# An attention and two-MoE kernel: first layer over pairs of groups, early attention products in four banks, k maximum by a tree, and all steps in one fixed list

## The chip, the cores and the metric

One core of a Trainium2 chip. The metric is the device time of one execution in microseconds (us), and the time of a kernel is the median of its runs. Five engines work side by side and wait for one another by semaphores: PE (TensorE, matmuls), DVE (VectorE), ACT (ScalarE), POOL (GpSimd) and SP (SyncE, which here issues nearly all DMAs, one after the other).

## What is computed

```python
# attention: q, k, v are 4 x 8 heads x 576 x 64, softmax of q over d, of k over the sequence
q_s = softmax(q, over d);  k_s = softmax(k, over seq)
x   = q_s @ (k_s.T @ v)                  # -> 2304 tokens x 512
# first MoE layer
h   = x @ w_in                           # 512 x 2048
g   = s * relu(h)**2 + b
x2  = g @ w_out                          # 2048 x 512
# second MoE layer: 8 experts, at most 576 tokens each, in token order
e   = argmax(x2 @ w_gate);  p = softmax weight of e
out = p * (relu(x2 @ w1[e]) @ w2[e])     # 0 for tokens over the capacity
```

## The kernel before

The 2304 tokens go in 9 groups of 256 (`G`), d_ff in 16 slices of 128 (`NF`). For the accuracy of fp32, every large product is three matmuls on high and low parts: high weight by high x, high weight by low x, low weight by high x. So each of the 16 slices of `w_in` and of `w_out` is loaded by SP (`load_w`, L181 and L186) and *converted*, in place, by six steps: `cv_abs` on ACT (L210), `cv_low` on DVE (L192), `cv_sign` on ACT (L202) or, for the slices listed in `bv`, on DVE (L200), `cv_join` on DVE (L215), `cv_hi` on ACT (L222) and `cv_lo` on DVE (L226).

**Attention.** For each of 4 batches and 4 pairs of heads: `load_k`, `k_max` (DVE, L351), transpose and maximum over partitions (`k_T` PE L358, `k_cm` DVE L364, `k_bc` PE L369), `k_sub` (DVE, or POOL for the pairs in `kpool`, L381), `k_exp` (ACT), the product k_s^T v (`k_kv`, PE L400), and the block `kvb` (`k_rec`, `k_blk`). For each group of tokens: `q_max`, `q_sub` (POOL), `q_exp`, `q_sum`, `q_norm` (POOL), transposes by PE (`q_T` L492, `q_Te`), `x1_mm` (PE, L507) for each half of the 512 columns, and its high and low parts `x1h`, `x1l` (`x1_hi` ACT L515, `x1_lo` DVE L521). In PSUM there are four banks of tag "x2", two of "h" and two of "a"; `x1_mm` uses an "a" bank.

**First MoE.** A unit is two blocks of 256 columns in one bank: for groups 0 and 1 the slices 2j and 2j+1 of one group, the two groups by turns; then group 2 alone, group 3 alone, and so on. `h_unit` is the first layer of a unit, 24 matmuls of 256 columns (L543 to L545). Then `h_relu` (ACT), `h_sq` (DVE), `h_hi` (ACT), `h_lo` (DVE), and two units later `x2_unit`, 12 matmuls of 512 columns (L609 to L611). Groups 0 to 3 (`NS`) get both layers. Groups 4 to 8 keep g and get the gate from `w_out` times `w_gate`, made once by the steps `w_add`, `w_tr`, `w_mm`, `w_x`, `w_sum`, `w_asm`, `w_shift`; x2 is then computed for tokens that are kept only (`x2_kept`, a branch).

**Second MoE.** The router's steps `r_*` give each token its slot. The first expert's weights are fetched ahead, and its first 256 tokens (part A) go through `gemm1_ahead` (L860 to L862) while the last group is routed. After that: the transposes of part B (`xpose_B`, PE L825), `gemm1` of part B, beside it the list of the other experts (`make_list`, some 25 small DVE steps) and the conversion of w2 (`conv2`, L782, by DVE and POOL in turn), then `gemm2` of both parts and the next expert. Nine DMAs fill the output with zeros (`zero_out`, L126).

What sets the order: every step has a rank, from its slot in a plan and hundreds of offsets (`PAR['d']`, `PAR['t']`). `arrange` (L1501) picks, engine by engine, the ready step that its model of costs lets start first, and emits the steps in that order; each engine then runs its own in that order. Where PE would wait, `arrange` puts idle matmuls (`warm`, L1599). What comes after the last `x2_kept` is written out by hand (L1626 to L1661).

Of the kernel before, what the change touches and what calls it, by code (L numbers as in the profile page):

```python
# [26 lines left out]
def kernel(ctx, tc, q, k, v, w_in, w_out, s_in, b_in, w_gate, w1, w2, cap, out, dbg=None):  # L27
    nc = tc.nc
# [29 lines left out]
    const = ctx.enter_context(tc.tile_pool(name="const", bufs=1))  # L58
# [198 lines left out]
    def w_mm(g, x2):
        if "ps" not in wx:
            wx["ps"] = ps_x.tile([P, 4, P], F32, tag="x2", name="pswg")
        for x in (x2, x2 + 1):  # L260
# [86 lines left out]
    def k_max(b, j):  # L347
        t = kt[b, j]
        p = P if b else P0
        m = at.tile([P, 2, D], F32, tag="rt", name="m1", bufs=2)  # L350
        nc.vector.tensor_reduce(out=m[:p], in_=t[:p].rearrange("p h r d -> p h d r"), axis=AX.X, op=ALU.max)  # L351
        kx[b, j] = m[:p].rearrange("p h d -> p (h d)")
# [147 lines left out]
    def x1_mm(n, hf):  # L500
        tt = qT.pop((n, hf))
        ps = ps_a.tile([P, 2, G], F32, tag="a", name="psx1")
        for i in range(2):
            for off, ln, b, s in runs(n):
                for r in range(2):
                    z = slice(r * D, (r + 1) * D)
                    nc.tensor.matmul(  # L507
                        ps[z, i, off:off + ln], kvb[b % 3][2 * hf + i][z], tt[z, i, off:off + ln],
                        start=True, stop=True, tile_position=(r * D, r * D),
                    )  # L510
        x1[n, hf] = ps
# [12 lines left out]
    def plan_q(n, s):
# [1215 lines left out]
```

## Time and profile before

| | |
|---|---|
| median of 3 runs | 563.48 us (562.38 to 563.79) |
| the profiled execution | 564.76 us, its span 563.0 us |
| PE busy | 539.3 us, 96% of the span |
| DVE, ACT, POOL busy | 320.6, 238.4, 132.6 us |
| HBM traffic | 59.97 MB, 107 GB/s over the span |

The profiled execution is 1.28 us above the median. Busy PE is not PE at its peak: idle matmuls and matmuls at a lower clock count as busy. The shares are means over stages with different limits, so the stages are read one by one.

### The profile page before, as it was taken

The page shows a single profiled execution, that of the slowest core. Times are in us where ns is not written, and L with a number is a line of the kernel's source. Part 1 is how long each engine was busy: PE and PEld are TensorE (multiplying, and loading weights), DVE is VectorE, ACT ScalarE, POOL GpSimd, SP SyncE. Part 2 cuts the span into 40 slices and gives each one's busy share as a digit, 9 for nine tenths or more (in the row PEclk, how much of TensorE's full clock was granted, in tenths as well). Part 3 has the DMA queues.
Part 4 walks back from the last instruction along what each step waited for, and adds up shares of the span by engine and source line. Part 5 has one row for each costly group of instructions (what it writes and reads, how often), then busy time and mean ns, then how long its engine had stood idle before and what let it go on. Part 6 is the DMA issues. An engine that isn't in the chain of part 4 may idle for free. (4 is left out here: it accounts for less than half of the span.)

```text
span 563.0 us, 10853 instructions
## 1 busy us (share of the span) xinstructions
PE 539.3 (96%) x4165; PEld 474.9 (84%) x4165; DVE 320.6 (57%) x735; ACT 238.4 (42%) x417; POOL 132.6 (24%) x184
## 2 busy tenths in 40 slices
PE   8999999999999999999999999999999878999993
PEld 8879988988888898888987989998899866899762
DVE  4999999993665575367464353473364557073010
ACT  2699898873423253224323322222352344162120
POOL 3400013122655222141211121140040206210111
PEclk9999999999999999999999999999999898999997
DMA  9996911314100652510100010103031899423101
GB/s 266 357 323 204 390 38 31 77 48 137 44 21 1 169 146 52 119 23 30 33 17 2 20 41 13 27 2 114 2 99 43 250 327 358 155 76 113 40 19 33
DMA packets 83333, 59.97 MB, mean 107 GB/s; under 512 B 40191, under 2 KB 75647, under 8 KB 83264
## 3 DMA queue, kind: packets, MB, share of 16 engines
q1 hardware_dynamic: 81104, 54.08, 31.7%
q0 software_dynamic: 2160, 5.01, 2.7%
q8 instruction: 39, 0.64, 0.5%
q14 instruction: 30, 0.25, 0.2%
HBM read 46.64 MB, written 12.51 MB: 105 GB/s over the span
## 5 line engine op out<-in xcount | busy, mean ns | idle before, releaser
L543 PE MATMUL psh<-x1h,wi 128*128 128x256 f32 x576 | 169.4, 294 | 1.3 <-PEq L644 0.7
L544 PE MATMUL psh<-x1l,wi 128*128 128x256 f32 x576 | 163.2, 283 | 0.3 <-DVE x1l L521 0.3
L545 PE MATMUL psh<-x1h,wi 128*128 128x256 f32 x576 | 162.9, 283 | 0.0
L543 PEld LDWEIGHTS psh<-x1h,wi 128*128 128x128 f32 x576 | 110.2, 191 | 9.3 <-issue 7.2
L544 PEld LDWEIGHTS psh<-x1l,wi 128*128 128x128 f32 x576 | 110.5, 192 | 1.0 <-DVE x1l L521 0.5
L545 PEld LDWEIGHTS psh<-x1h,wi 128*128 128x128 f32 x576 | 110.3, 191 | 0.0
L609 PE MATMUL psx<-wo,gh 128*128 128x512 f32 x128 | 52.0, 406 | 0.0
L573 DVE SCALAR_TENSOR_TENSOR rt<-rt,sb_s 128x512 f32<-128x512 f32 x44 | 36.8, 836 | 26.5 <-ACT rt L565 26.5
L610 PE MATMUL psx<-wo,gh 128*128 128x512 f32 x128 | 50.3, 393 | 0.0
L611 PE MATMUL psx<-wo,gl 128*128 128x512 f32 x128 | 50.1, 391 | 0.0
L565 ACT ACTIVATE rt<-psh 128x512 f32<-128x512 f32 x44 | 26.3, 599 | 56.2 <-PE psh L545 53.1
L247 POOL TENSOR_TENSOR wS<-wo 128x128 f32<-128x128 f32 x64 | 31.7, 526 | 30.6 <-DVE wT L254 30.6
L565 ACT ACTIVATE rg<-psh 128x512 f32<-128x512 f32 x28 | 16.6, 598 | 45.7 <-PE psh L545 36.7
L762 POOL DMA_INDIRECT mapd<-rpay,rslot x18 | 18.9, 1052 | 49.5 <-DMA mapd<-rpay,rslot 19.4
L573 DVE SCALAR_TENSOR_TENSOR rg<-rg,sb_s 128x512 f32<-128x512 f32 x28 | 20.9, 752 | 16.5 <-ACT rg L565 16.5
L466 POOL TENSOR_TENSOR qt<-qt,qm 128x512 f32<-128x512 f32 x14 | 17.6, 1277 | 48.7 <-DVE qm L458 34.3
L782 DVE TENSOR_TENSOR W<-raw,W 128x512 fp32r<-128x512 f32 x28 | 22.6, 830 | 11.0 <-ACT W L781 10.3
L609 PEld LDWEIGHTS psx<-wo,gh 128*128 128x128 f32 x128 | 24.3, 190 | 5.3 <-issue 1.0
L611 PEld LDWEIGHTS psx<-wo,gl 128*128 128x128 f32 x128 | 24.1, 188 | 5.3
L351 DVE TENSOR_REDUCE m<-kt 128x128 f32<-128x640 f32 (+1 forms) x16 | 21.6, 1352 | 11.2 <-DMA kt<-in_k 8.3
L610 PEld LDWEIGHTS psx<-wo,gh 128*128 128x128 f32 x128 | 24.2, 189 | 4.3 <-DVE wo L226 0.3
L959 POOL DMA_INDIRECT out<-y,mp x11 | 10.6, 965 | 70.4 <-ACT y L958 56.8
(226 smaller groups left out, 1113.3 us busy)
## 6 DMA issues: line engine op xcount, KB each, us to landing
ri<-in_moe_w_in SPq DMA_DIRECT2D x16, 512.0 KB, 8.2
ro<-in_moe_w_out SPq DMA_DIRECT2D x16, 512.0 KB, 10.1
raw<-in_moe_w SPq DMA_DIRECT2D x12, 512.0 KB, 5.8
raw<-in_moe_w SPq DMA_DIRECT2D x24, 256.0 KB, 4.9
out<-zero SPq DMA_DIRECT2D x9, 512.0 KB, 6.4
kt<-in_k SPq DMA_DIRECT2D x12, 256.0 KB, 3.1
vt<-in_v SPq DMA_DIRECT2D x24, 128.0 KB, 2.8
x2d<-zero SPq DMA_DIRECT2D x5, 512.0 KB, 3.3
```

What stands on the lines that cost most here:

```text
L247: nc.gpsimd.tensor_tensor(t[:, c], hi, lo, ALU.add)
L351: nc.vector.tensor_reduce(out=m[:p], in_=t[:p].rearrange("p h r d -> p h d r"), axis=AX.X, op=ALU.max)
L543: nc.tensor.matmul(ps, wt[:, 0, o], xh[:, c % 2], start=(c == 0), stop=False)
L544: nc.tensor.matmul(ps, wt[:, 0, o], xl[:, c % 2], start=False, stop=False)
L545: nc.tensor.matmul(ps, wt[:, 1, o], xh[:, c % 2], start=False, stop=(c == NC - 1))
L565: nc.scalar.activation(t, ps, AF.Relu)
L573: nc.vector.scalar_tensor_tensor(t, t, sb_s, t, op0=ALU.mult, op1=ALU.mult)
L609: nc.tensor.matmul(ps, gh[:, i, o], wt[:, 0], start=(f == 0), stop=False)
L610: nc.tensor.matmul(ps, gh[:, i, o], wt[:, 1], start=False, stop=False)
L611: nc.tensor.matmul(ps, gl[:, i, o], wt[:, 0], start=False, stop=(f == NF - 1))
L762: nc.gpsimd.indirect_dma_start(out=mapd[:, :], out_offset=bass.IndirectOffsetOnAxis(ap=slot[:, t:t + 1], axis=0), in_=pay[:, t], in_offset ...
L782: eng.tensor_tensor(dst[:, 1], src, dst[:, 0].bitcast(F32), ALU.subtract)
```

## The change

- **Pairs of groups.** For groups 0 to 3 a unit is one slice of `w_in` by two groups: `h_unit` is 12 matmuls of 512 columns. `x1h` and `x1l` of two groups lie in one tile (three buffers each). The first unit needs the x1 of groups 0 and 1; `x2_unit` holds four banks at a time.
- **Start.** `x1_mm` of groups 0 and 1 takes "x2" banks. SP loads k before q, and two k tiles of the next batch early. `k_max` is three `tensor_tensor` steps (L356 to L358).
- **Conversions.** 13 signs by DVE instead of 9; 10 `k_sub` on POOL instead of 6. `w_mm` in four parts in "a" banks.
- **One fixed list.** `arrange` takes the steps in the order of `PAR['seq']`. The list now also has what was written by hand: the evictions of part A's `gemm1_ahead`, the transposes of part B, its `gemm1_B0`, the making of the list, `conv2_0`, and the next expert's fetch and gather. The `zero_out` DMAs stand early.
- **End.** The last `gemm2` of part A of the second expert is held in a bank, and its output is written in both branches that follow; the experts after the second ("rest") are one general path.

```diff
+    XB = 3
+    PAIRED = (0, 1, 2, 3)
+    half_of = {n: n % 2 if n in PAIRED else 0 for n in range(NG)}
...
-        m = at.tile([P, 2, D], F32, tag="rt", name="m1", bufs=2)
-        nc.vector.tensor_reduce(out=m[:p], in_=t[:p].rearrange("p h r d -> p h d r"), axis=AX.X, op=ALU.max)
+        m = at.tile([P, 3, 2, D], F32, tag="rt", name="m1", bufs=2)[:p]
+        t = t[:p].rearrange("p h r d -> p r h d")
+        x = 2 if b else 3
+        nc.vector.tensor_tensor(m[:, 0:x], t[:, 0:x], t[:, x:2 * x], ALU.max)
+        nc.vector.tensor_tensor(m[:, 0], m[:, 0], m[:, 1], ALU.max)
+        nc.vector.tensor_tensor(m[:, 0], m[:, 0], t[:, 4] if b else m[:, 2], ALU.max)
...
-        ps = ps_a.tile([P, 2, G], F32, tag="a", name="psx1")
+        ps = ps_x.tile([P, 2, G], F32, tag="x2", name="psx1") if n < 2 else ps_a.tile([P, 2, G], F32, tag="a", name="psx1")
...
     def x1_hi(n, hf):
-        xh = at.tile([P, 2, G], F32R, tag="x1h", name="x1h", bufs=4)
-        nc.scalar.activation(xh, x1[n, hf], AF.Copy)
+        z = half_of[n]
+        if z == 0:
+            shape = [P, 2, 2 if n in PAIRED else 1, G]
+            xs[n, hf] = [at.tile(shape, F32R, tag=f"x1{y}", name=f"x1{y}", bufs=XB) for y in "hl"]
+        xs[n, hf] = xs[n - z, hf]
+        nc.scalar.activation(xs[n, hf][0][:, :, z], x1[n, hf], AF.Copy)
...
     def h_unit(u, pair):
-        for i in range(2):
-            h_half(u, pair, i)
+        gs[u] = ps_h.tile([P, 2, G], F32, tag="h", name="psh")
+        h_mm(gs[u], *pair[0])
...
-    for j in range(NF // 2):
-        for n in range(2):
-            units.append([(2 * j, n), (2 * j + 1, n)])
-    for n in range(2, NG):
+    for n in PAIRED[::2]:
+        units_of[n] = units_of[n + 1] = list(range(len(units), len(units) + NF))
+        units += [[(f, n), (f, n + 1)] for f in range(NF)]
+    for n in range(NS, NG):
...
+    def gemm1_B0(f, ps=None):
...
+    def list_step(z):
+        if z == 0:
+            late["list"] = make_list()
+        next(late["list"], None)
+
+    def fetch_1():
+        load_e(1)
+        load_map(1)
+        for z in range(4):
+            load_raw1(1, z, *((wpi, f"wi{z}") if z < 2 else (late["moe"], f"raw{z}")))
...
     def arrange(steps):
...
+        place = {label: z for z, label in enumerate(PAR["seq"])}
...
-        while todo:
-            best = {}
...
+        for key in sorted(todo, key=lambda x: todo[x][0]):
             rank, f, a, work, after, takes, gives = todo.pop(key)
...
-        near("stale")
-        listing = make_list()
-        for f in range(NF2):
-            if tilesB:
-                gemm1(0, f, *items[0]["xB"], *hB(0, f))
-            if listing:
-                for _ in range((1, 2, 2, 9)[f]):
-                    if next(listing, 1):
-                        listing = None
-                        load_e(1)
-                        fetch_A(1)
-                        break
-            conv2(0, f, nc.gpsimd if f % 2 else nc.vector)
```

SP at the start, the first loads of the program, before (`kt`, `qt`, `vt` are tiles of k, q and v, `ri` and `ro` slices of `w_in` and `w_out`):

```order
L442 DMA qt<-in_q 128x8x128 x2
L310 DMA kt<-in_k 96x2x384 x4
L181 DMA ri_153<-in_moe_w_in 128x4x256
L181 DMA ri_155<-in_moe_w_in 128x4x256
L331 DMA vt<-in_v 96x2x384
```

and now:

```order
L313 DMA kt<-in_k 96x2x384 x3
L449 DMA qt<-in_q 128x8x128
L313 DMA kt<-in_k 96x2x384
L184 DMA ri_172<-in_moe_w_in 128x4x256
L184 DMA ri_176<-in_moe_w_in 128x4x256
L449 DMA qt<-in_q 128x8x128
L334 DMA vt<-in_v 96x2x384 x2
```

Three k tiles are issued before the first q, and the second q stands behind two slices of `w_in`.

PE just ahead of the first matmul of the first layer (`psh`), before (`psq` transposes of q, `psx` products that give x1):

```order
L1599 MATMUL warm<-ident 128x128
L492 MATMUL psq<-ident,qe 128x128 x4
L1599 MATMUL warm<-ident 128x128 x4
L492 MATMUL psq<-ident,qe 128x128 x4
L507 MATMUL psx_451<-qT,kvb_2_109 64x256 x2
L507 MATMUL psx_451<-qT,kvb_3_110 64x256 x2
L1599 MATMUL warm<-ident 128x128 x3
L507 MATMUL psx_466<-qT,kvb_0_107 64x256 x2
L507 MATMUL psx_466<-qT,kvb_1_108 64x256 x2
L543 MATMUL psh<-x1h,wi_435 128x256
```

and now:

```order
L514 MATMUL psx_444<-qT,kvb_0_107 64x256 x2
L514 MATMUL psx_444<-qT,kvb_1_108 64x256 x2
L499 MATMUL psq<-ident,qe 128x128 x4
L514 MATMUL psx_458<-qT,kvb_2_109 64x256 x2
L514 MATMUL psx_458<-qT,kvb_3_110 64x256 x2
L365 MATMUL psk<-ident,m_423 128x128
L514 MATMUL psx_471<-qT,kvb_2_109 64x256 x2
L514 MATMUL psx_471<-qT,kvb_3_110 64x256 x2
L1727 MATMUL warm<-ident 128x128
L407 MATMUL pskv<-vt,kt 64x65 x10
L554 MATMUL psh<-x1h,wi_387 128x512
```

All four x1 products, and one k product of the next batch, stand ahead of the first layer; the fourth x1 product stood behind the first unit before. One idle matmul is left among them.

SP at the end of the first expert's loads, before (`raw` are pieces of w1 and w2, `out` the output, `mp` a map of tokens):

```order
L793 DMA raw_6198<-in_moe_w 128x512
L126 DMA out<-zero 1024x1x128 x9
L1223 TENSOR_LOAD first_i
L1621 TENSOR_LOAD list_i
L800 DMA mp<-mapd 128x5x4
L786 DMA raw_6349<-in_moe_w 128x4x256
```

and now:

```order
L655 UNCONDITIONAL_BRANCH
L1161 TENSOR_LOAD list_i
L817 DMA mp<-mapd 128x5x4
L797 DMA raw_6048<-in_moe_w 128x4x256
```

No zeros stand there any more, and the read of the list and the next expert's loads follow directly on the last branch of `x2_kept`, while `gemm1_B0` is still ahead on PE.

## Rows read from the trace of the kernel before

**Rows 1.** The page: busy time of each engine, its share and instructions.
```profile
PE 539.3 (96%) x4165; PEld 474.9 (84%) x4165; DVE 320.6 (57%) x735; ACT 238.4 (42%) x417; POOL 132.6 (24%) x184
```
**Rows 2.** Busy time by stage: start:end, length, engines (instructions), PE clock, DMA share, GB/s.
```profile
0.00:35.01 35.01, 32.29 (x295) 28.70 (x295) 25.82 (x44) 19.29 (x30) 13.16 (x36) 1.00 0.99 316
35.01:136.00 100.99, 100.64 (x718) 88.77 (x717) 90.90 (x153) 82.84 (x127) 14.50 (x17) 1.00 0.49 149
437.95:472.32 34.37, 27.88 (x153) 24.71 (x153) 22.14 (x61) 14.34 (x30) 11.71 (x10) 0.90 1.02 324
```
**Rows 3.** PE's timeline at the start: start, duration, line, operation, count, idle before.
```profile
1.64 11.56 PE L1599 MATMUL warm<-ident 128*128 128x128 f32 x78 [1.64 <-POOL ident masks.py:199]
13.04 0.25 PE L358 MATMUL psk<-ident,m 96*128 96x96 f32 x1
...
28.50 0.65 PE L507 MATMUL psx<-qT,kvb 64*64 64x256 f32 x4 [0.44 <-ACT kvb L414]
...
31.53 0.66 PE L492 MATMUL psq<-ident,qe 128*128 128x128 f32 x4
...
35.01 0.39 PE L543 MATMUL psh<-x1h,wi 128*128 128x256 f32 x1
...
38.06 1.08 PE L507 MATMUL psx<-qT,kvb 64*64 64x256 f32 x8
```
**Rows 4.** DVE's timeline at the start.
```profile
6.37 1.22 DVE L458 TENSOR_REDUCE qm<-qt 128x16 f32<-128x1024 f32 x1 [0.54 <-DMA qt<-in_q]
7.56 2.94 DVE L351 TENSOR_REDUCE m<-kt 96x128 f32<-96x768 f32 x2
13.32 1.51 DVE L351 TENSOR_REDUCE m<-kt 96x128 f32<-96x768 f32 x1 [2.82 <-PE psk L358]
...
18.10 2.67 DVE L381 TENSOR_TENSOR kt<-kt,psb 96x768 f32<-96x768 f32 x3
...
25.30 2.13 DVE L215 SCALAR_TENSOR_TENSOR cT<-cT,ri 128x512 int32<-128x512 int32 x1
```
**Rows 5.** POOL's timeline at the start.
```profile
24.98 1.90 POOL L484 TENSOR_TENSOR qe<-qe,qs 128x1024 f32<-128x1024 f32 x1 [0.40 <-DVE rec L408]
```
**Rows 6.** PE's timeline inside the first layer and the second: starts of matmuls of 256 and 512 columns.
```profile
36.77 0.28 PE L545 MATMUL psh<-x1h,wi 128*128 128x256 f32 x1
...
37.85 0.28 PE L545 MATMUL psh<-x1h,wi 128*128 128x256 f32 x1
...
133.05 0.48 PE L609 MATMUL psx<-wo,gh 128*128 128x512 f32 x1
133.36 0.40 PE L610 MATMUL psx<-wo,gh 128*128 128x512 f32 x1
...
135.64 0.39 PE L611 MATMUL psx<-wo,gl 128*128 128x512 f32 x1
```
**Rows 7.** DVE's groups, 35 to 136 us: busy, mean ns, idle before.
```profile
L215 DVE SCALAR_TENSOR_TENSOR cT<-cT,ro 128x512 int32<-128x512 int32 x16 | 11.7, 734 | 1.6 <-ACT ro L202 1.5
L200 DVE TENSOR_SCALAR ro<-ro 128x512 uint16<-128x512 uint16 x5 | 3.8, 753 | 0.0
L381 DVE TENSOR_TENSOR kt<-kt,psb 128x640 f32<-128x640 f32 x2 | 1.6, 804 | 0.0
```
**Rows 8.** PE's timeline after the last block of gemm1_ahead: two of its waits.
```profile
441.54 0.46 PE L825 MATMUL psg<-ident,xg 64*128 64x64 f32 x4 [1.04 <-DVE xB L832]
...
466.61 0.50 PE L944 MATMUL pso<-W,hA 128*128 128x512 f32 x1 [3.19 <-POOL W L782]
```
**Rows 9.** Busy time in two stretches of that stage, columns as in rows 2.
```profile
444.00:448.00 4.00, 4.00 (x19) 4.00 (x18) 1.56 (x6) 0.95 (x2) 0.83 (x1) 0.57 1.00 321
468.00:472.00 4.00, 4.00 (x15) 3.14 (x14) 4.00 (x6) 1.21 (x3) 3.54 (x3) 0.59 1.04 402
```
**Rows 10.** SP's and POOL's timelines in that stage.
```profile
442.10 14.80 SPq L126 DMA_DIRECT2D out<-zero  x9
465.28 3.75 POOL L782 TENSOR_TENSOR W<-raw,W 128x512 fp32r<-128x512 f32 x3
```

More of the change, by code (lines that the diff above doesn't have):

```diff
@@ L255, in w_tr, with w_mm @@
         wx[g, x] = t
[L257 to L260, printed above, removed]
+    def w_mm(g):
+        ps = ps_a.tile([P, P], F32, tag="a", name="pswg")
+        for x in range(4):
             t, d = wx.pop((g, x)), wx["g"]
@@ L952, in gemm2 @@
             ps = y
-        y_out(i, t, m, ps)
+        if not held:
+            y_out(i, t, m, ps)
     def y_out(i, t, m, ps):
@@ L1146 @@
     main.append((x2_kept, NG - 1))
+    if tilesB:
+        for f in range(NF2):
+            main.append((gemm1_B0, f))
     first, last = {}, {}
@@ L1366, in parts @@
             for c, n in pair:
-                gives += [((x1_hi, n, hf), "x1") for hf in range(2) if c == NF - 1]
+                gives += [((x1_hi, n, hf), "x1") for hf in range(2) if c == NF - 1 and not half_of[n]]
                 gives += [((cv_hi, ("i", c)), f"wi{c}")] if u == last_unit(c) else []
@@ L1423, in parts @@
             n = a[0]
-            work = [("PE", 0.5)] + [(e, 0.2) for e in EVERY[1:]]
+            us = KEPT.get(n, 0.0)
+            work = [("PE", 0.5 + us), ("ACT", 0.2 + us), ("DVE", 0.2 + us), ("POOL", 0.2), ("SP", 0.2 + us)]
             after = [(r_keep, n)] + [(h_sq, u) for u in units_of[n]]
@@ L1445, in parts @@
             work, after, takes = [("POOL", 4.2)], [(load_map, 0), (x2_kept, nL - 1)], ["rt"] * len(tilesA)
+            after += [(zero_out, t) for t in range(NT // 256)]
         elif f is gather_B:
@@ L1517, in arrange @@
-            todo[key] = (rank, f, a, work, after, takes, gives)
+            label = ":".join([f.__name__] + ["".join(map(str, y)) if isinstance(y, tuple) else str(y) for y in key[1:]])
+            todo[key] = (place[label], f, a, work, after, takes, gives)
             for g in gives:
                 owed[g] = owed.get(g, 0) + 1
-        for key, row in todo.items():
-            for x in row[4]:
-                assert x in todo, (key, x)
-        todo = dict(sorted(todo.items(), key=lambda x: x[1][0]))
@@ new lines, in arrange @@
+        for key in sorted(todo, key=lambda x: todo[x][0]):
+            rank, f, a, work, after, takes, gives = todo.pop(key)
+            eng = work[0][0] if work else ""
+            t = max([free.get(eng, 0)] + [end[x][0] + (0.1 if end[x][1] == eng else 0.2) for x in after])
+            for tag in takes:
+                ring = held.get(tag, [])
+                z = len(ring) + takes.count(tag) - 1 - many.get(tag, 1)
+                if z >= 0:
+                    back = freed.get((ring[z], tag), [])
+                    assert 0 < len(back) == owed.get((ring[z], tag)), (key, tag)
+                    t = max(t, max(back) + 0.2)
+            if f in (x2_kept, cand_state):
+                t = max([t, free.get("PE", 0)] + [free.get(e, 0) + 0.8 for e in ("ACT", "DVE")])
@@ L1668 @@
                     xpose_B(0, tile_)
-                gemm1_B(0)
+                for f in range(NF2):
+                    gemm1_B0(f, late["psB"])
+        if tilesB:
+            gemm1_ev(late["psB"], *hB(0, NF2 - 1))
         def when(i, least, f):
```

396 lines of the change are left out of this document (230 added, 166 removed).

## The prediction

> **What bounds the kernel now.** I read the page first: PE is busy 96% of the span [rows 1]. That share hides where time can be had, so I then read the stages one by one [rows 2]. Three matter here. Up to 35.01 us PE has nothing to multiply: its busy time is idle matmuls and attention products, until the first matmul of the first layer (`psh`, L543) starts at 35.01 [rows 3]. From 35.01 to 136.00 PE has no gap (100.64 of 100.99 us), but DVE is busy 90.90 and ACT 82.84, because all 32 weight slices are converted there. From 437.95 to 472.32, between the first expert's part A and the next expert, PE is busy 27.88 of 34.37 us at a mean granted clock of 0.90, with the DMA engines full (share 1.02). Elsewhere PE simply has work, and the change leaves that work as it is.
>
> All sums are against the profiled execution, 564.76 us, span 563.0; the median, 563.48, is 1.28 below it. I take the change of the one for that of the other.
>
> **The start: -8.2 us.** What is removed, from rows 3 and 4:
> - The first pair of k maxima ends at 7.56 + 2.94 = 10.50, yet its transpose starts at 13.04, since PE works off 78 idle matmuls from 1.64 on; the third maximum then waits 2.82 us for PE. Now 22 matmuls (11 in the order, two records each) stand there: 22 x 11.56 / 78 = 3.3 us, ending at 4.9, before a k tile can have landed. Worth 2.5.
> - Four maxima take 4 x 1.48 = 5.9 us of DVE. The tree is 384 + 128 + 128 columns; the nearest row of two tiles is the subtraction of 768 columns, 2.67 / 3 = 0.89, so 640 columns are 0.74; the fixed part of two more instructions stands in no row alone, and I take 0.1 each: 0.95. Worth 4 x 0.5 = 2.0. Ends: 0 (three steps as dear as one reduction) and 3.0 (0.74 flat).
> - k landed behind both q: DVE takes up q until 7.56. Now three k tiles come first. The second q and its POOL steps then end later, so I count 0 net; ends -1 and +2.
> - With two "a" banks the x1 products wait for evictions: between 28.50 + 0.65 = 29.15 and 31.53 PE does one set of transposes (0.63) and idle matmuls. Four banks let the products follow each other. Worth 2.4 - 0.6 = 1.8, of which I take 1.5, as the new products wait for the second q in part.
> So the first layer starts 6.0 earlier, at about 29.0. The fourth x1 product (1.08 at 38.06) and one k product of similar length, which stood behind the first unit, are now ahead of it: 2.2 more. Ends for the whole: 4 and 10.
>
> **The pairs: -4.3 us.** Inside a block 256 columns start every (37.85 - 36.77) / 9 = 0.120 us, 512 columns every (135.64 - 133.36) / 10 = 0.228 [rows 6]. A unit of 24 x 0.120 = 2.88 becomes 12 x 0.228 = 2.74: 0.14. Groups 0 to 3 have 32 units either way, so 4.5 us. The first matmul of a block lasts longer in both forms (0.31 to the next at 133.05); I take 4.3. Ends: 0, if the new form ran like two matmuls, and 4.6. The row ahead of this is the reason for the upper end: the same width, on the same engine, in the same stage.
> [...]
>
> **DVE and ACT under the pairs: +2 us.** PE's work from the first unit to the end of groups 0 and 1 falls from 100.6 to 100.6 - 2.2 - 16 x 0.135 = 96.2. DVE's 90.90 changes so [rows 7]: 4 signs more, 4 x 0.75 = +3.0; 4 `k_sub` fewer, 4 x 0.80 = -3.2; q of group 3 now falls into this stage (its maximum and sum, each like the 1.22 of rows 4, the sum's two small steps, and two x1l, each like the join of rows 7: 2 x 1.2 + 0.4 + 2 x 0.7 = +4.2); one conversion more behind the first unit, since it starts earlier, four steps, of which join and sign are 0.73 and 0.75, about +2.4; and of six k maxima at 1.4 to 1.5 [rows 4] two come earlier and four are cheaper, 2 x 1.4 + 4 x 0.43 = -4.5. Sum +1.9, so 92.8 of 96.2. That still fits, but with 3% of slack and steps that must come in order, so I add 2 us of waiting on PE (ends 0 and 7). ACT loses four signs and is not the bound.
> One row speaks against putting four more `k_sub` on POOL: the join of L215, 0.73 us in the mean [rows 7], took 2.13 at 25.30 [rows 4] while POOL's `q_norm` ran from 24.98 to 26.88 [rows 5], and it ended 0.55 after that. If each of the four cost DVE as long as that `q_norm`, 4 x 1.9 = 7.6 us, DVE would stand at 100.4 against 96.2 and PE would wait 4.2 us, with the 2 above some 6 to 7: that is the upper end.
> [...]
>
> **Between the pairs: +1 us.** Groups 2 and 3 need x1 of both ahead of their first unit, and the third x1 buffer is the only free one; the second half waits for the last unit of groups 0 and 1. Two second-layer units (2 x 2.74) hide its evictions (some 3.5 us). Ends 0 and 3.
>
> **The stage before the second expert: -8.3 us.** PE idles 34.37 - 27.88 = 6.5 us, and in 444 to 448 and 468 to 472 the granted clock is 0.57 and 0.59 with PE busy all the time [rows 9]: 4 x 0.43 + 4 x 0.41 = 3.4 us lost, at the 1.2 GHz level for most of it, after the waits of 1.04 [rows 8] and 3.19. Sum 9.9. What ends the waits goes: part B is transposed while `gemm1_ahead` still has blocks; nine zero DMAs, 14.80 us of issue [rows 10], no longer stand ahead of the next expert's loads; the list is made earlier; and the 3.19 came from POOL's three conversions of w2 in 3.75 us, which were late because their loads were. What is late next is `gemm1_B0` itself, 14 us of PE work, which covers the 4 x 512 KB of w1 and the gather. I leave 1.6. Ends: -4 (the loads still collide) and -10. The zeros cost nothing where they go now: DMA share falls to 0.49 after the start [rows 2], and SP's next loads there are needed tens of us later.
>
> Other edits (cheaper branches at the end, the held bank, `w_mm` by parts) I count at nothing: PE has other work there.
>
> **Sum:** -8.2 - 4.3 + 2 + 1 - 8.3 = -17.8. 564.76 - 17.8 = 547.0 for a profiled execution, **545.7** for the median.
>
> **Rivals.**
> 1. *DVE becomes the bound of the first pair.* For: 92.8 of 96.2 and the 2.13. Against: now PE idles only 0.35 us in all that stage [rows 2]. Price: 5 more waiting and half the start's 8.2 eaten: 563.48 - 17.8 + 5 + 4 = 555.
> 2. *The zeros and k loads, moved into the full DMA stage (share 0.99), delay weights and the start.* The start gives nothing; 563.48 - 9.6 = 554.
> 3. *The end doesn't do what it says:* the list or the gather is late in its new place and PE still falls to 1.2 GHz. The stage gives 2 of 8.3: 552.
> 4. *The pairs give a quarter.* If the wide matmuls of the first layer started every 0.237 us and not every 0.228, a unit would save 2.88 - 12 x 0.237 = 0.04 and all of them 1.1: 545.7 + 3.2 = 549. Rows 6 speak against it, with the same width in the second layer. [...]
> 5. *Slower: the fixed list makes each second-layer unit wait for its g.* In the first 32 units the chain relu, square, high, low is four steps of ACT and DVE on 512 columns, each like the 0.73 of the join [rows 7], some 2.9 us, behind conversions in both queues. Between a unit's first and second layer lie two more of each, 4 x 2.74 = 11 us. If conversions ahead of the chain hold it longer than that, each unit pays; at 0.8 us x 32 = 26 the result is 545.7 + 26 = 571. It decides from 17.8 / 32 = 0.56 us a unit. Against: with the same chain and the same lag PE idles 0.35 us in that stage now [rows 2].
>
> **How the numbers follow.** The forecast, 0.60, holds about 540 to 550; rivals 1 to 3 together 0.25; rival 4 0.04; a result better than 540, with every term at its far end, 0.06; rival 5 0.05. The range 538 to 555 leaves out the slow rival and most of the better case; rivals 1 to 4 and the forecast's own ends lie inside. About 0.3%, 1.7 us, is what a measurement can tell from no change. All cases but rival 5 are faster by more: faster 0.93, same 0.02, slower 0.05.
>
> **What would show it.** Right: the first `psh` matmul, now 512 wide, near 29 us, 12 of them in 2.7 us; groups 0 and 1 done near 128; no clock below 0.9 and under 2 us of PE idle time around part B's `gemm1`. Wrong: PE waits for `x1l`, `wi`, `wo` or `gl` between 30 and 130 (rivals 1, 2, 5); a granted clock of 0.6 near the list (rival 3); 512 columns at 0.24 (rival 4).

## The result, and the profile after

The change made the kernel a little slower, by 0.75%: 567.25 us in the median (564.64 to 570.27) against 563.63 for the kernel before beside it (560.87 to 565.03), a ratio of 1.0075 (1.0047 to 1.0102). Two repeats gave 1.0062 (1.0038 to 1.0085) and 1.0037 (1.0022 to 1.0052). I had forecast 545.7, in a range of 538 to 555. The profiled execution's span went from 563.0 to 567.3.

The page of the changed kernel, busy time, answers to [rows 1]:

```profile
PE 531.6 (94%) x3735; PEld 450.5 (79%) x3735; DVE 326.1 (57%) x767; ACT 233.6 (41%) x420; POOL 146.8 (26%) x189
```

PE has 430 instructions and 7.7 us of work less. So the span grew by PE's idle time. Busy time by stage of the changed kernel, columns as in [rows 2]; the stages are cut at the same marks as in the table below:

```profile
0.00:37.91 37.91, 30.83 (x280) 26.28 (x280) 32.35 (x55) 19.47 (x33) 17.13 (x38) 0.95 0.96 273
37.91:142.56 104.65, 101.08 (x519) 79.14 (x515) 101.86 (x177) 80.92 (x127) 26.15 (x28) 0.98 0.58 181
142.56:307.14 164.58, 159.89 (x1250) 133.74 (x1248) 89.42 (x258) 55.12 (x110) 49.61 (x76) 1.00 0.23 60
...
406.11:451.81 45.70, 40.18 (x288) 36.45 (x288) 26.05 (x79) 16.35 (x35) 10.41 (x10) 0.93 0.25 71
451.81:468.19 16.38, 14.24 (x98) 14.01 (x97) 7.48 (x18) 7.10 (x16) 8.31 (x7) 1.00 0.58 212
468.19:560.70 92.51, 88.27 (x506) 73.47 (x506) 25.18 (x53) 27.34 (x53) 14.04 (x15) 0.98 0.28 89
```

Each stage's length, beside the same cut of the kernel before and what the prediction's terms come to there. Some 36 matmuls of the last group's first layer (4.3 us at 0.12) now run before the first x2 of group 4 and not after group 7; the column "like for like" moves them back.

| stage (its end) | before | after | like for like | forecast |
|---|---|---|---|---|
| first `psh` | 35.01 | 37.91 | +2.9 | -6.0 |
| second layer of groups 0 and 1 done | 100.86 | 104.65 | +3.8 | -2.4 |
| first second-layer matmul of group 4 | 161.65 | 164.58 | -1.4 | -1.2 |
| the same of group 7 | 100.76 | 98.97 | -1.8 | 0 |
| first `psy<-xB` | 44.19 | 45.70 | +5.8 | -8.3 for this |
| first `pso` | 18.38 | 16.38 | -2.0 | and the next |
| last matmul | 92.65 | 92.51 | -0.1 | two |
| end of span | 9.5 | 6.6 | -2.9 | 0 |

Three places hold the miss: the start by 8.9, groups 0 and 1 by 6.2, and the three rows from group 7 to the last matmul, taken together, by 12.0.

**The start.** PE's first steps in the changed kernel (answers to [rows 3]):

```profile
1.53 4.82 PE L1727 MATMUL warm<-ident 128*128 128x128 f32 x22 [1.53 <-POOL ident masks.py:199]
6.18 0.25 PE L365 MATMUL psk<-ident,m 96*128 96x96 f32 x1
```

DVE's timeline, then POOL's (answers to [rows 4, 5]):

```profile
4.21 0.55 DVE L356 TENSOR_TENSOR m<-kt 96x384 f32<-96x384 f32 x1 [4.21 <-DMA kt<-in_k]
4.80 0.29 DVE L357 TENSOR_TENSOR m<-m 96x128 f32<-96x128 f32 x1
...
10.24 3.36 DVE L356 TENSOR_TENSOR m<-kt 96x384 f32<-96x384 f32 x1
13.64 1.77 DVE L357 TENSOR_TENSOR m<-m 96x128 f32<-96x128 f32 x1
...
18.03 1.21 DVE L465 TENSOR_REDUCE qm<-qt 128x16 f32<-128x1024 f32 x1
```

```profile
9.19 1.81 POOL L388 TENSOR_TENSOR kt<-kt,bc 96x768 f32<-96x768 f32 x1 [7.72 <-DVE cm L371]
...
11.14 2.05 POOL L473 TENSOR_TENSOR qe<-qt,qm 128x512 f32<-128x512 f32 x2
13.15 2.11 POOL L388 TENSOR_TENSOR kt<-kt,bc 96x768 f32<-96x768 f32 x1
...
27.17 1.90 POOL L491 TENSOR_TENSOR qe<-qe,qs 128x1024 f32<-128x1024 f32 x1 [2.78 <-DVE cm L371]
```

The same step of the tree takes 0.55 at 4.21 and 3.36 at 10.24, while POOL works through a `k_sub` and two halves of `q_sub`; the next, 1.77 in place of 0.29, ends 0.15 after POOL's second `k_sub`. So the second q's maximum stands at 18.03, and its `q_norm` at 27.17 where it was at 24.98 [rows 5].

**Groups 0 and 1.** DVE and POOL of the changed kernel where PE first waits long:

```profile
71.26 2.04 DVE L229 TENSOR_TENSOR wi<-cT,wi 128x512 fp32r<-128x512 f32 x1
...
74.94 1.54 DVE L584 SCALAR_TENSOR_TENSOR rt<-rt,sb_s 128x512 f32<-128x512 f32 x1
...
84.04 2.39 DVE L606 SCALAR_TENSOR_TENSOR gl<-rt,sb_b,gh 128x512 fp32r<-128x512 f32 x1
```

```profile
71.03 1.71 POOL L388 TENSOR_TENSOR kt<-kt,bc 128x640 f32<-128x640 f32 x1 [22.15 <-ACT bc L384]
74.50 2.88 POOL L473 TENSOR_TENSOR qt<-qt,qm 128x512 f32<-128x512 f32 x2 [1.77 <-DVE qm L465]
83.72 2.17 POOL L491 TENSOR_TENSOR qt<-qt,qs 128x1024 f32<-128x1024 f32 x1 [6.33 <-DVE qs L486]
```

The DVE steps that begin beside these POOL steps end a little less than their own length after them: 73.30 is 0.56 after POOL's 72.74, 86.43 is 0.54 after 85.89. In [rows 4, 5] it was 0.55. PE pays behind it (ACT's `rt` had waited 1.62 us for that `gl`), and again at half clock (granted 0.50 of full speed from 88.3 to 91.0: 0.63 for 512 columns, which take 0.39 at 1.00):

```profile
87.19 0.50 PE L554 MATMUL psh<-x1h,wi 128*128 128x512 f32 x1 [1.55 <-ACT rt L576]
...
88.52 0.63 PE L555 MATMUL psh<-x1l,wi 128*128 128x512 f32 x1
```

**The end.** DVE's timeline and PE's, from the last group's logits on ("remote" is a release that the profile ties to no instruction of the program):

```profile
430.04 0.68 DVE L849 TENSOR_TENSOR xA<-psg,xA 128x512 fp32r<-128x512 f32 x1
433.94 0.48 DVE L698 TENSOR_SCALAR lt<-psl,shift 128x256 f32<-128x256 f32 x1 [3.22 <-remote]
```

```profile
434.48 1.02 PE L704 MATMUL psL<-sum,lt 128*128 128x8 f32 x4 [4.30 <-DVE lt L698]
...
468.19 0.47 PE L979 MATMUL pso<-W,hA 128*128 128x512 f32 x1 [2.14 <-PEq L1752]
...
537.42 0.47 PE L979 MATMUL pso<-W,hB 128*128 128x512 f32 x1 [4.23 <-issue]
```

The waits of [rows 8, 9] are gone: no 3.19 for W and no half clock near 444 or 468 (granted 1.00 from 444 to 448 and from 468 to 472). Three new ones stand there: 4.30 for `lt`, 2.14, and 4.23 of "issue", where PE waits for nothing that the profile shows, at the branch "full", the one that chooses the path behind the second expert's part A.

### The profile page after: what moved, and what is told of

Its sections match the earlier page's. It is cut to its first block, busy times and chain, and to the rows that moved or that the text cites. A ratio compares the mean times of both kernels' runs of the same rounds, so it can differ in the third digit from the quotient of the medians.

```text
span 567.3 us, 10042 instructions
## 1 busy us (share of the span) xinstructions
PE 531.6 (94%) x3735; PEld 450.5 (79%) x3735; DVE 326.1 (57%) x767; ACT 233.6 (41%) x420; POOL 146.8 (26%) x189
## 5 line engine op out<-in xcount | busy, mean ns | idle before, releaser
L554 PE MATMUL psh<-x1h,wi 128*128 128x256 f32 (+1 forms) x448 | 146.5, 327 | 2.7 <-ACT rt L576 1.6
L556 PE MATMUL psh<-x1h,wi 128*128 128x256 f32 (+1 forms) x448 | 141.1, 315 | 0.1
L555 PE MATMUL psh<-x1l,wi 128*128 128x256 f32 (+1 forms) x448 | 141.1, 315 | 0.0
L554 PEld LDWEIGHTS psh<-x1h,wi 128*128 128x128 f32 x448 | 85.6, 191 | 12.8 <-issue 4.6
L556 PEld LDWEIGHTS psh<-x1h,wi 128*128 128x128 f32 x448 | 85.6, 191 | 6.0 <-DVE wi L229 0.7
L555 PEld LDWEIGHTS psh<-x1l,wi 128*128 128x128 f32 x448 | 85.8, 191 | 4.9 <-DVE x1l L533 0.2
L584 DVE SCALAR_TENSOR_TENSOR rt<-rt,sb_s 128x512 f32<-128x512 f32 x44 | 35.3, 807 | 17.8 <-ACT rt L576 17.7
L388 POOL TENSOR_TENSOR kt<-kt,bc 128x640 f32<-128x640 f32 (+1 forms) x10 | 17.8, 1777 | 90.4 <-ACT bc L384 82.6
L250 POOL TENSOR_TENSOR wS<-wo 128x128 f32<-128x128 f32 x64 | 34.6, 571 | 18.4 <-DVE wT L257 18.4
L473 POOL TENSOR_TENSOR qt<-qt,qm 128x512 f32<-128x512 f32 x14 | 17.8, 1289 | 83.1 <-DVE qm L465 69.7
L584 DVE SCALAR_TENSOR_TENSOR rg<-rg,sb_s 128x512 f32<-128x512 f32 x28 | 22.6, 833 | 14.6 <-ACT rg L576 14.5
L606 DVE SCALAR_TENSOR_TENSOR gl<-rt,sb_b,gh 128x512 fp32r<-128x512 f32 x32 | 27.4, 857 | 6.0 <-ACT gh L597 6.0
```

What stands on the lines that cost most here:

```text
L250: nc.gpsimd.tensor_tensor(t[:, c], hi, lo, ALU.add)
L388: eng.tensor_tensor(t, t, bc, ALU.subtract)
L554: nc.tensor.matmul(ps, wt[:, 0, o], xh[:, c % 2], start=(c == 0), stop=False)
L555: nc.tensor.matmul(ps, wt[:, 0, o], xl[:, c % 2], start=False, stop=False)
L556: nc.tensor.matmul(ps, wt[:, 1, o], xh[:, c % 2], start=False, stop=(c == NC - 1))
L584: nc.vector.scalar_tensor_tensor(t, t, sb_s, t, op0=ALU.mult, op1=ALU.mult)
```

## The experiments

A sitting here is a set of kernels run one after another on the same chip with the kernel before beside them (the expectations say "call"). Each of the five sittings of these experiments was on another chip. The kernel before gave 563.05 to 564.58 in all of them, so times compare across sittings within some 1.5 us, but for one stall that is followed below. Ends of groups 0 and 1 given in the text are the start of the last matmul: 142.3 in the change.

**Subtractions of the k maximum on DVE.** The one edit:

```diff
- 'kpool': ((0, 2), (0, 3), (1, 0), (1, 1), (1, 2), (1, 3), (2, 2), (3, 0), (3, 1), (3, 3))
+ 'kpool': ()
```

> The changed kernel with all 16 k_sub on DVE and none on POOL, in the same list. Theory (a POOL instruction on two SBUF tiles holds up DVE's two-tile instructions): of the ten k_sub on POOL, six lie before the end of groups 0 and 1, 11.5 us of POOL work; DVE gets six steps of 0.8 to 0.95 us, 5 us, and is freed of most of the 11.5. The fourth k transpose comes from 15.9 to about 13, the first psh from 37.9 to 35 or 36, groups 0 and 1 end 4 to 6 us sooner than 142.6, total about 562 (0.998 of the kernel before). Rival (DVE is simply full of its own work): DVE gets 8.5 us more, groups 0 and 1 end 4 to 5 us later, total about 571. Rival (loads set the pace): no change, within 1 us.

561.98, ratio 0.9966 (0.9949 to 0.9984). DVE was given ten more subtractions and the kernel became 5.3 us faster than the change. By stage:

```profile
0.00:36.45 36.45, 30.55 (x293) 26.35 (x294) 31.08 (x59) 18.81 (x29) 11.90 (x35) 1.00 0.95 280
36.45:137.30 100.85, 98.76 (x519) 78.21 (x516) 98.36 (x179) 80.60 (x125) 21.20 (x25) 1.00 0.61 189
```

The start is 1.5 shorter and the stage of groups 0 and 1 3.8, the whole of what it had lost. It is DVE's time that fell, 101.86 to 98.36, with the work added to it: three of the ten subtractions lie in that stage (6.0 us on POOL, 2.4 on DVE).

**The k maximum by one reduction.** The three steps of L356 to L358 go back to one `tensor_reduce`.

```diff
-        nc.vector.tensor_tensor(m[:, 0:x], t[:, 0:x], t[:, x:2 * x], ALU.max)
...
+        nc.vector.tensor_reduce(out=m[:p], in_=t[:p].rearrange("p h r d -> p h d r"), axis=AX.X, op=ALU.max)
```

> The changed kernel with k_max as one reduction again, in the same list. Theory (the tree's steps read two SBUF tiles and wait for POOL, a reduction reads one and does not): the fourth k maximum takes 1.5 us in place of 5.2 (10.24 to 15.44), its transpose starts near 12 in place of 15.9, the first psh near 34 to 35 in place of 37.9; the later maxima cost 1.3 in place of 0.9 plus holds, about even. Total 563 to 565. Rival (the tree is cheaper, the start waits for loads of v and q): the first psh stays within 0.5 us of 37.9 and DVE's ten maxima before 142.6 cost 4 us more: total 570.

563.71, 0.9999 (0.9973 to 1.0025), 3.5 below the change. The start fell to 35.22, by 2.7; the stage after it, 104.58, did not move. So the tree loses time in the start alone, where POOL's steps stand beside it.

**The branch as it was.** Two things go back at once, the hint ahead of the products of part A and the plain form of the branch without `preferred_fallthrough_block`; the runs do not tell them apart.

```diff
             late["pso"] = ps_h.tile([P, DM], F32, tag="h", name="pso")
+            near("full")
...
-            with tc.If(regs["c", 1] < MARK, label="full", preferred_fallthrough_block=False):
+            with tc.If(regs["c", 1] < MARK, label="full"):
```

> The changed kernel with the branch at the end as it was before: its hint ahead of gemm2 of part A and no preferred_fallthrough_block. Theory (the 4.2 us that PE stands still at 533 to 537 are the fetch of code behind an unhinted branch): that wait falls to about 0.8 as in the kernel before, total 3.4 us less, about 564. Rival (PE waits there for the held bank's output or a load): the wait stays at 3 to 4 us, total unchanged at about 567.

560.89, 0.9952 (0.993 to 0.9974), 6.4 below the change where 3.4 was expected. The 4.23 of "issue" became

```profile
530.97 0.47 PE L979 MATMUL pso<-W,hB 128*128 128x512 f32 x1 [0.58 <-PEq L1808]
```

and the stretch from the first `pso` to the last matmul 87.3 us at a clock of 1.00, where the change has 92.5 at 0.98 and the kernel before 92.65. In the kernel before, whose branch has this form too, PE waits 0.83 there. That the 4 us are a fetch of code was not shown: no row of the trace says what PE did in them. So the 3.19 and the half clock of [rows 8, 9] had been won, some 5 us, and the branch gave them back.

**First layer by 256 columns.** `h_unit` issues 24 matmuls of 256 columns over the same tiles and order.

```diff
-        h_mm(gs[u], *pair[0])
+        for i in range(2):
...
+                nc.tensor.matmul(ps, wt[:, 0, o], xh[:, c % 2], start=(c == 0), stop=False)
```

> The changed kernel whose first layer of groups 0 to 3 goes by 256 columns again, 24 matmuls for 12, over the same pair of groups and in the same list. Theory (512 columns save 0.14 us a unit wherever PE is the bound; in groups 0 and 1 DVE is the bound and hides it): groups 2 and 3, from 142.6 to 258.3, take 2.3 us more, groups 0 and 1 less than 1 us more; total +2.5 to +3.5, about 570. Rival (the pairs give their 4.5 us everywhere): +4.5, about 572. Rival (they give nothing): no change.

568.87, 1.01 (1.0066 to 1.0134), 1.6 above the change where 2.5 to 3.5 was expected. Groups 0 and 1 end at 142.1, about as with 512 columns: there PE's time is not what sets the end. Groups 2 and 3 take 1.9 more, where PE does: some 0.12 for each of their 16 units; I had taken 0.14. Summed from start to start, with steps over 0.35 us (waits and half clock) counted at their usual length, the first layer of groups 0 to 3 takes PE 94.6 us before, 94.7 here, 90.5 in the change and 90.1 in the joined version below: 4.1 and 4.5 less; I had forecast 4.3.

**Zero writes late, and the stall ahead of `lt`.** Five `zero_out` moved behind `zero_out:4` in the list:

```diff
- 'zero_out:0' ... 'zero_out:3' ... 'zero_out:7' ... 'zero_out:6' ... 'zero_out:2'
+ 'zero_out:4', 'zero_out:0', 'zero_out:3', 'zero_out:7', 'zero_out:6', 'zero_out:2'
```

> The changed kernel with its five early zero writes (in SP's list among the weight loads of the first 130 us) moved behind the sixth-last group, where DMA has room; nothing else is moved. Theory (POOL's two-tile instructions hold DVE up while DVE is the bound of groups 0 and 1): no load is waited for by PE there, so the time stays at 567 within 1.5 us, and groups 0 and 1 end at 142 within 1. Rival (DMA share of 1.0 up to 80 us makes weights late, and PE and DVE wait for them): groups 0 and 1 end 4 to 7 us earlier, at 135 to 138, and the time is 560 to 563.

562.56, 0.9982 (0.9965 to 1.0): as the rival had it by the total, but not by the place. Groups 0 and 1 ended at 141.29, 1.0 earlier. The rest came from the end, where `lt` did not wait:

```profile
431.21 0.47 DVE L698 TENSOR_SCALAR lt<-psl,shift 128x256 f32<-128x256 f32 x1
```

**The register read late.** `cand_state`, each engine's read of a flag, moved to just ahead of the list:

```diff
- 'h_sq:70', 'cand_state', 'h_sq:64'
+ 'x2_kept:8', 'cand_state', 'list_step:0'
```

> The changed kernel with cand_state (each engine reads a flag from SBUF into a register) moved from ahead of the last group's logits to just ahead of list_step. Theory A (the 3.2 us that DVE waits ahead of lt of the last group, and the 4.3 that PE waits behind it, are this register read): both waits fall below 1, the clock stays near 1.00 from 430 to 440, and the time falls by about 3 to 564, unless the read costs the same in its new place, where PE has gemm1_ahead to do. Rival B (the wait is for something else, such as the logits' own matmuls or their weight): the wait of lt stays at 3 to 4.3 and the time at 567 within 1.5.

563.78, 1.0019 (0.9989 to 1.0049), and no wait: it looked like theory A.

**All subtractions on POOL.**

```diff
- 'kpool': ((0, 2), (0, 3), (1, 0), (1, 1), (1, 2), (1, 3), (2, 2), (3, 0), (3, 1), (3, 3))
+ 'kpool': ((0, 0), (0, 1), (0, 2), (0, 3), (1, 0), ..., (3, 3))
```

> The changed kernel with all 16 subtractions of the k maximum on POOL, where the change has 10 there and an earlier run of this study none. Theory (each one holds DVE up for its time, about 1.6 us, and takes only 0.8 off DVE's own work): of the six that move, four stand ahead of the end of groups 0 to 3's weight conversion; groups 0 and 1 end later, at 143 to 147, and the time is 567 to 573. From none to 10 the time rose by 5.3; by the same slope 16 gives about 570. Rival (the fixed list lost time for another reason and POOL's part relieves DVE): groups 0 and 1 end earlier than 142 and the time is below 566.

561.7, 0.9969 (0.9947 to 0.9991): my total was wrong. The stages ahead of it were not far off: the start went to 38.97, groups 0 and 1 ended at 143.1, at the low edge of what I wrote (of the six that move only two lie ahead of that point, both in the start). Again the gain lay behind group 7, and the wait of `lt` was missing.

**Joined.** No subtraction on POOL, one reduction, the branch as it was: the three edits above together.

> The changed kernel with three of its parts taken back at once: no subtraction of the k maximum on POOL, the k maximum by one reduction, and the hint for the branch at the end ahead of the last products. By themselves these gave -5.3, -3.5 and -6.4 against 567.25. If they are separate costs, as the theory has it: 567.25 - 15.2 = 552, and up to 556 since the first two are both paid in the start and in groups 0 and 1. Rival (all three shorten one and the same wait, or a run-to-run shift explains them): 559 to 562, no better than the best one alone. Kernel before: 563.5.

548.39, 0.9744 (0.971 to 0.9778): faster than both kernels and than the sum of the parts, 552. Here too `lt` did not wait. All four kernels of this sitting lacked that wait (one profiled execution each); the change and the four variants run before all had it. A cause in the kernels' text would have had to be struck four times by four unlike edits.

**The change again, and a block to fill the wait.**

> The changed kernel once more, unaltered, as a control: in the runs so far DVE's wait of 3.2 us ahead of the last group's lt stood in the changed kernel and in four variants that ran beside it or before, and was absent in all four of a later call, though one of them had altered only SP's order. Theory A (that wait goes with the execution or the chip and not with the kernel's text): this run shows no such wait, and a time of about 563.5, 3 to 4 below 567.25. Theory B (it goes with the kernel's text): the wait of 3 to 4 is there again and the time is 567 within 1.5.

567.32, with the wait (4.29 on PE).

```diff
- 'r_lt:8', 'r_back:8', 'conv1:0:1', 'gather_B', 'gemm1_ahead:0'
+ 'r_lt:8', 'gemm1_ahead:0', 'r_back:8', 'conv1:0:1', 'gather_B'
```

> The changed kernel with the first block of gemm1_ahead (12 or 24 matmuls of 256 columns, some 3 us) moved ahead of r_back of the last group, so that PE has it to do while DVE makes lt, as in the kernel before. If the stall of PE there is 4.3 as in the changed kernel's first profile, it covers 2.9 of it and keeps the clock: -3 to -4 against the control of this call. If the stall is 1.0 as in the later runs, it covers that: -1, within 1. Rival (lt and the list then come later by the block and delay the scatter and gather that the next stage waits for): +1 to +3, with PE waiting for xB or psg.

565.6, 1.0042 (1.0018 to 1.0067), 1.7 below its control, the intervals overlapping; PE's wait halved:

```profile
434.23 0.61 PE L704 MATMUL psL<-sum,lt 128*128 128x8 f32 x4 [2.13 <-DVE lt L698]
```

**The tree without `k_sub` on POOL.** The joined version with L356 to L358 as the change has them.

> As the joined version (548.39: no subtraction on POOL, k maximum by one reduction, the hint back), but with the change's tree for the k maximum. It tells what the tree is worth once POOL's subtractions are off the first 16 us. Theory (the tree is held up by any POOL instruction with two tiles, and q_sub still runs beside the fourth maximum): slower than 548.4, by 1 to 4, with the fourth k transpose at 13 to 14 and groups 0 and 1 ending at 136 to 138. Rival (the tree saves its 0.5 us each once k_sub is gone): 546 to 548, with the fourth transpose ahead of 13.2.

555.9, 0.9858 (0.982 to 0.9896), with the wait of `lt`; 2.9 above the joined version in the same sitting (552.99, below), so the tree costs that much, as expected; 2.4 of it lie in the start (37.28 against 34.91). The fourth maximum of this run on DVE, and POOL:

```profile
11.88 0.55 DVE L356 TENSOR_TENSOR m<-kt 96x384 f32<-96x384 f32 x1
12.46 1.02 DVE L357 TENSOR_TENSOR m<-m 96x128 f32<-96x128 f32 x1
13.51 1.02 DVE L358 TENSOR_TENSOR m<-m 96x128 f32<-96x128 f32 x1
```

```profile
12.05 2.34 POOL L473 TENSOR_TENSOR qe<-qt,qm 128x512 f32<-128x512 f32 x2 [10.34 <-DVE qm L465]
```

The two short steps take 1.02 each beside the two halves of `q_sub`. In the joined version the reduction in the same place is not held up, beside the same POOL steps:

```profile
11.55 1.50 DVE L354 TENSOR_REDUCE m<-kt 96x128 f32<-96x768 f32 x1
```

```profile
11.72 2.05 POOL L469 TENSOR_TENSOR qe<-qt,qm 128x512 f32<-128x512 f32 x2 [10.01 <-DVE qm L461]
```

**The joined version with that block.**

> The joined version (548.39) with the first block of gemm1_ahead ahead of r_back of the last group as well. The joined version's PE waits 0.99 for psL's lt and 1.51 for hA after that. If the block covers the first: 547, within 1. Rival, as for the block alone: 549 to 551.

552.99, 0.9829 (0.9785 to 0.9873), with the wait. This kernel lacked the move: it is the joined version unaltered, and tells only that this version is 4.6 slower in a sitting with the wait.

**Text or sitting.** Four kernels again, unaltered, in one sitting.

> The joined version a second time, unaltered. Theory A (DVE's 3.2 us ahead of lt goes with the call, that is with the chip or its state, and moves every variant of the change alike while the kernel before, which has multiplications to do there, does not feel it): if the control of this call shows the wait, this run shows it too and stands at 552 to 553; if the control shows none, it stands at 548.4 again. Theory B (it goes with the kernel's text): no wait and 548.4 within 1, whatever the control shows.

> The version with cand_state late a second time, unaltered. Theory A: the wait stands here if it stands in this call's control, and the time is then 567 to 568, no better than the control. Theory B (moving the register read removed it): no wait, and 3.5 below the control.

> The version with the zero writes late a second time, unaltered. Theory A: as the control as to the wait, and 1.0 below it, since its groups 0 and 1 ended 1.0 earlier. Theory B: no wait, and 4.7 below the control.

> The changed kernel a third time, as the control of this call. Theory A allows either: the wait and 567, or no wait and 563.5. Theory B: the wait and 567 within 1.

552.21, 566.38, 567.54 and 566.5, and a wait ahead of `lt` in all four. With the zero writes late, groups 0 and 1 end at 142.1, in the control at 142.5: the zero writes are not what holds that stage. With the register read late the wait is shorter, but the time is that of the control:

```profile
432.48 0.48 DVE L698 TENSOR_SCALAR lt<-psl,shift 128x256 f32<-128x256 f32 x1 [1.67 <-issue]
```

Theory A holds: the stall goes with the sitting. It shifted the joined version by 4, the zero writes by 5.0 and the register read by 2.6; the kernel before not at all (563.78 and 563.05 without, 563.49 to 564.58 with it). The register read is not its cause: in the run above DVE reads the flag at 440.4, behind `lt`, and `lt` waits all the same. The zero writes and the register read are then worth nothing, and 561.7 for all subtractions on POOL belongs beside some 563, what the change itself would give without the stall. That last number is an estimate (567.3 less 4); the changed kernel was not run in such a sitting, and the 1.6 between the two are too few to call a gain. The six subtractions more cost nothing that this run shows; four of them lie behind groups 0 and 1, where DVE has slack (89.42 busy of 164.58 in the change). The stall was there on three chips (4, 5 and 14) and not on two others (8 and 10), one sitting on each, so sitting and chip can't be told apart; the cause is open.

**The block again, beside its control.**

> The joined version with the first block of gemm1_ahead between r_lt and r_back of the last group (in the run named best that move was missing from the kernel, which was the joined version once more). In the changed kernel the same move shortened PE's wait for lt from 4.29 to 2.13 and the time by 1.7 (565.60 against 567.32). If the stall stands in this call: 550.5 to 552 and 1 to 2 below this call's joined version, with PE's wait near 2. If it does not: 547.5 to 549, level with it. Rival (the joined version's DVE reaches the list too late for it): 1 to 2 above it.

> The joined version again, as the control of this call: 552 to 553 with the 3 us wait of lt, or 548.4 without it.

548.66 and 548.24, without the wait in either. The block neither helps nor hurts there; whether it covers the stall in the joined version stays open.

## Why the prediction was wrong

The joined version shows best which terms held. It runs the change's pairs, list and banks; busy time by stage, cut as above:

```profile
0.00:34.66 34.66, 30.65 (x294) 26.43 (x294) 29.88 (x47) 18.59 (x29) 11.34 (x35) 1.00 0.96 286
34.66:135.85 101.19, 99.00 (x518) 78.09 (x515) 99.25 (x171) 80.64 (x125) 21.01 (x25) 1.00 0.62 191
135.85:298.42 162.57, 159.92 (x1249) 133.79 (x1247) 88.05 (x251) 53.96 (x106) 43.18 (x72) 1.00 0.24 61
...
397.42:437.90 40.48, 37.98 (x288) 34.32 (x288) 25.76 (x79) 16.36 (x35) 10.44 (x10) 1.00 0.25 71
437.90:452.29 14.39, 14.24 (x98) 14.01 (x97) 7.01 (x18) 7.10 (x16) 6.68 (x5) 1.00 0.74 252
452.29:539.75 87.46, 86.87 (x506) 72.87 (x506) 25.63 (x54) 27.34 (x53) 16.09 (x16) 1.00 0.30 97
```

**The start, -8.2: wrong.** The warm-up term held: the first k transpose moved from 13.04 [rows 3] to 6.18, though the 22 idle matmuls took 4.82 us and not 3.3, and a k tile had landed by 4.21, ahead of their end. The tree saves 0.36 a maximum undisturbed (4.21 to 5.33 is 1.12, against 1.48), not 0.5, and the fourth took 5.5. The step that failed is "the second q and its POOL steps then end later, so I count 0 net". From the end of the second `q_norm` to the first `psh` lie 8.1 us before (26.88 to 35.01), 8.8 in the change (29.07 to 37.91) and 9.0 in the joined version (25.65 to 34.66): in all three the first layer follows the second q at about the same distance. That it is what sets the start is read from this and was not tested alone. What stands in that distance now holds the fourth x1 product and a k product, 2.0 us more than before, for 0.7 to 0.9 us, so the term of the four banks (1.5) and the work moved ahead (2.2) about held. The start gained 0.35 in the joined version, not 6.0, and lost 2.9 in the change. DVE is busy 29.88 of 34.66 there. The second `q_norm` of the joined version:

```profile
23.75 1.90 POOL L487 TENSOR_TENSOR qe<-qe,qs 128x1024 f32<-128x1024 f32 x1 [1.26 <-DVE cm L367]
```

**DVE under the pairs, +2: mis-sized, and its upper end was the truth.** I gave DVE 92.8 us of work; it has 101.86 of 104.65. The groups of the changed kernel in that stage, answering to [rows 7]:

```profile
L606 DVE SCALAR_TENSOR_TENSOR gl<-rt,sb_b,gh 128x512 fp32r<-128x512 f32 x16 | 15.4, 964 | 0.2 <-ACT gh L597 0.2
L218 DVE SCALAR_TENSOR_TENSOR cT<-cT,ro 128x512 int32<-128x512 int32 x15 | 12.5, 841 | 0.1
L218 DVE SCALAR_TENSOR_TENSOR cT<-cT,ri 128x512 int32<-128x512 int32 x13 | 11.2, 861 | 0.0
L229 DVE TENSOR_TENSOR wi<-cT,wi 128x512 fp32r<-128x512 f32 x14 | 11.0, 792 | 0.0
L257 DVE STREAM_TRANSPOSE wT<-wS 128x128 f32<-128x128 f32 x8 | 1.8, 275 | 0.0
```

Before, `gl` had a mean of 738 ns, the join of `ro` 734 and of `ri` 749, `wi` 686. By these means the holding up costs 16 x 0.226 + 15 x 0.107 + 13 x 0.112 + 14 x 0.106 = 8.2 us, less 1.9 on `wo` (844 to 727): 6.3. That is not far from the 7.6 that I had priced as an upper end (four times the 1.9 of [rows 5]) and then set aside, but the reason given for it was not the one. POOL's groups in this stage, before:

```profile
L381 POOL TENSOR_TENSOR kt<-kt,bc 128x640 f32<-128x640 f32 x3 | 5.1, 1714 | 38.4 <-ACT bc L377 38.4
L247 POOL TENSOR_TENSOR wS<-wo 128x128 f32<-128x128 f32 x4 | 3.0, 769 | 0.0
```

and in the change:

```profile
L250 POOL TENSOR_TENSOR wS<-wo 128x128 f32<-128x128 f32 x12 | 8.7, 751 | 6.0 <-DVE wT L257 6.0
L388 POOL TENSOR_TENSOR kt<-kt,bc 128x640 f32<-128x640 f32 x3 | 6.0, 2010 | 51.4 <-ACT bc L384 51.4
```

There are three `k_sub` on POOL in either kernel. What grew is `w_add` (`wS`), twelve for four, and q, two groups for one: POOL is 26.15 us busy for 14.50 [rows 2]. My sum of DVE's work had two slips besides: it took four `k_sub` off DVE (-3.2) where [rows 7] has two (1.6), and it left out the eight transposes of `w_tr` that came into the stage (L257, 1.8 us). With an engine at 97% of a stage, every microsecond of this is paid. Rival 1 was right as to this place. Even in the joined version DVE has 99.25 of 101.19, so the pairs' 2.2 us do not show in this stage.

**What holds DVE.** In the traces above DVE steps that read two tiles of SBUF beside POOL's two-tile steps (2.13 for a join of 0.73 [rows 4, 5, 7], 2.04 at 71.26 for the `wi` of 0.69), and also the one-tile `tensor_scalar` of L195 (0.42 us alone, 2.01 at 27.34 beside POOL's 27.17), are held until POOL's instruction ends; they end 0.55, 0.56 and 0.28 after it. The reduction is not: 1.50 at 11.55 beside the halves of `q_sub`, 1.51 at 13.32 [rows 4] with POOL idle. What in the engines does this, and why L195 is held and the reduction is not, both with one input, no row shows. The 3.36 at 10.24 shows besides that one DVE step can be held by more than one POOL instruction: it began beside the `k_sub` that ended at 11.00 and ended behind both halves of `q_sub`, at 13.60.

**The pairs, -4.3: right,** in PE's own time (4.1 and 4.5) and where PE is the bound. Rival 4 falls: no run shows its 0.237 us; in the change the first layer's matmuls of 512 columns start every 0.227 us (2.50 from 163.94 to 166.44 for 11 of them). **Between the pairs, +1:** with what follows, -1.4 against -1.2.

**The stage before the second expert, -8.3: right as to what goes, wrong as to what is late next.** In the joined version the last three stages, like for like, give +0.6 - 4.0 - 5.2 = -8.6. In the change they give +3.7. The 12.3 between are three stalls: 5.2 at `lt` with the half clock behind it (45.70 against 40.48; granted 0.50 from 434.4 to 439.0), 2.0 ahead of the first `pso`, 5.05 at the branch. "I count at nothing" failed for the branch: one edit to it cost what the new order had won. The `lt` stall I could not see: the order itself, by running the last group's blocks and transposes earlier, as I read it, leaves PE with nothing at that point, where the kernel before went on with `gemm1_ahead`. That the kernel before is alike in all sittings agrees with this; the block put back halved the wait, but its 1.7 us are within what the intervals allow for chance. So why DVE stalls there stays open; what the runs show is its price, some 3 to 5 us. The 2.14 came and went between runs, and I have no cause for it. Nor was it tested why the span ends 2.9 sooner behind the last matmul. What the prediction calls the 1.2 GHz level is in the trace of the kernel before a granted clock of 0.50 of full speed (444 to 447 and 468 to 471), with a matmul of 320 columns every 0.267 us (444.35 to 447.02), 1.20 columns a ns; a frequency stands in no row.

**The joined version's total was partly luck.** In a sitting without the stall it stands 15.4 below the kernel before (548.39 against 563.78), near the 17.8 of the forecast, but the start's 6.0 are not in it, and 2.9 behind the last matmul, which I had at nothing, are.

**The other rivals.** Rival 2's zero writes were tested and are not it; its k loads were not tested. Rival 3's low clock came (0.50 from 88.3 and from 434.4 on in the change), behind other waits than the list's. **The slower rival** (second-layer units waiting for g, 571) did not happen as told: PE waits for `gl` once, 0.7 us. The time was reached by other ways, and some 4 us of it by the stall: by the estimate of 563 the change would be level with the kernel before without it. I gave 0.05 to all slower cases, since I added the gains at their likely values and most dangers singly, as rivals; here three of them came together.

## What to carry to other kernels

Before moving two-input work to POOL, ask not what DVE is relieved of but how much slack DVE has in that stage: each such POOL step can stop DVE for most of its length. The 1.71 us at 71.03 cost DVE 1.36 and had saved it some 0.8. A reduction that reads one tile is then better than a shorter tree of two-input steps: here by 2.9 us. When an order is packed tighter, list what PE had to do at each late result; a stall that other work had covered becomes visible. And price an edit to a branch from a row, or test it: this one was worth some 5 us, more than the pairs.

## What the runs showed of the hardware that I had not expected

- A stall of DVE ahead of one instruction (3.1 to 3.2 us, but 1.7 and 2.4 in one run each) was there in every variant of the change in some sittings and in none in others, each sitting on another chip; the same joined kernel took 552.21 and 552.99 with it, 548.39 and 548.24 without. A single comparison of two variants in different sittings would have credited it to an edit, as it did here for three of them.
- PE spent some 4 us at a branch without the hint ahead of it and with another fall-through (3.87 to 4.60 over the runs that have it so), and 0.58 with both put back.
- DVE's 96-partition maximum of 384 columns, 0.55 us, took 3.36 when a `k_sub` and two halves of `q_sub` followed one another closely on POOL.
